# Loading and multiplying the gate matrix ahead of the query matrix in a one-token attention and GEGLU kernel

## The chip, the core and the metric

The kernel runs on one core of one Trainium2 chip. The metric is device time in microseconds (us) of one execution; lower is better. A core has a tensor engine (PE, with its weight loads shown apart as PEld), a vector engine (DVE), a scalar engine (ACT), a GpSimd engine (POOL) and a sync engine (SP). In this kernel SP only issues transfers from memory, in the order in which the program lists them, and 16 DMA engines carry them out.

## The reference, cut to what matters

Eight tokens (one for each batch entry, 512 wide) are normalised, and the normalised `xn` goes two ways. One is attention over the last 1024 positions of a cache of 8 key/value heads, with 32 query heads of 128. The other is a GEGLU block with 1792 hidden columns. The second gates the first.

```
xn = layernorm(x)                                   # 8 x 1 x 512
q  = xn @ wq                                        # 512 x 4096
p  = softmax(q . k_cache[last 1024] * 128**-0.5)    # 8 batches, 8 kv heads
s  = (p @ v_cache[last 1024]) @ wo                  # 4096 x 512
g  = silu((gelu(xn @ w_gate) * (xn @ w_up)) @ w_down)
out = x + s * g
```

All tensors are bf16. Key and value windows are 2 MB for each head, so 32 MB of them are read; `wq` and `wo` are 4 MB each, and `w_gate`, `w_up` and `w_down` are 1.8 MB each. That is 47.5 MB read for a very small amount of arithmetic for each byte.

## The kernel before, in words

**Buffers and transfers.** Every large operand lands in one of nine equal buffers called `big` (16 KB in each of 128 partitions, L69). They are used in turn, so the tenth tile takes the buffer of the first, and its transfer waits until the first tile has been read for the last time. All of these transfers are issued by SP in program order: `wq` in three transfers (L141 to L150: rows k=0, k=1, and k=2 and 3 together), then the gate matrix, the up matrix, key heads 0 to 2, the down matrix, value head 0, and from then on key and value heads in turn, last `wo` in seven pieces. `load_rows` (L92) loads a whole weight matrix with four consecutive rows for each partition: for the gate and up matrices this is one run of 4 x 1792 bf16 values, 14336 bytes, in each partition. A row of `wq` is a run of 8192 bytes; the third `wq` transfer has runs of 16384 bytes. The small input `x` is issued by ACT (L90).

**The opening.** `x` is normalised on DVE and ACT (L176 to L188), turned into columns on PE (L194), and copied into two padded layouts: `xqT`, by DVE (L197), which the query products use, and `xnT`, by ACT (L201), which the gate and up products use. Then come the query products (L311), 32 matmuls into two PSUM tiles `sc` and `o_ps`, in the order of the four row groups k; two casts each by DVE (L318) and ACT (L322) into `q_row`; `spread_x` (L218), which puts `x` into the layout of the output; the gate products (L359, w = 0), 16 matmuls into PSUM tile `s`; `turn_queries` twice (L328), 16 transposes on PE and eight copies in turn by DVE and ACT into `qT`; `masks` (L254) on DVE; and the up products (L359, w = 1) into `o_ps`. All of it stands in one hand-written order; each engine runs its instructions in that order.

**The loop.** L578 runs over steps of half a set (a set is half a head's batches): keys are transposed on PE (L439) and copied out by DVE and ACT in turn (L450, L452), scores are formed (L461), softmax follows (L469 to L504), values are multiplied nine steps later (L515), and `gather` (L526) normalises a head. The GELU of the gate result is spread over the first loop steps (`hidden_steps`, L374), two of its operations a step. `wo` is multiplied last (L621, L629), and the output is formed by two DVE operations (L657, L658).

**Transfer waits.** A transfer on SP also waits for the eighth transfer before it (that on ACT counted) to have landed, beside the wait for its buffer.

Of the kernel before, what the change touches and what calls it, by code (L numbers as in the profile page):

```python
# [12 lines left out]
FP32 = mybir.dt.float32  # L13
# [4 lines left out]
def kernel(  # L18
# [13 lines left out]
    nc = tc.nc  # L32
# [7 lines left out]
    F = B_w_gate.shape[1]  # L40
    NDC = D // 128
    NFC = F // 128
    scale = float(Dh) ** -0.5
    P = nc.NUM_PARTITIONS
# [17 lines left out]
    NQB = D // 128  # L62
# [15 lines left out]
    ps_o = ctx.enter_context(tc.tile_pool(name="ps_o", bufs=1, space=PSUM))  # L78
    ps_s = ctx.enter_context(tc.tile_pool(name="ps_s", bufs=1, space=PSUM))
# [12 lines left out]
    def load_rows(w, r0, n, per, name):  # L92

        t = big.tile([P, 2 * SET], BF16, name="big")
        cols = w.shape[1]
        nc.sync.dma_start(  # L96
            out=t[:, 0 : n * cols],
            in_=w.rearrange("(p k) n -> p k n", p=P)[:, r0 : r0 + n, :],
        )
        return t[:, 0 : n * cols].rearrange("p (k n) -> p k n", k=n)  # L100
# [24 lines left out]
    def load_wo(h, r0, n, nh=1):  # L125

        t = wo_at(h)[:, h % HB : h % HB + nh, r0 * D : (r0 + n) * D]
        nc.sync.dma_start(
            out=t if nh > 1 else t[:, 0, :],
            in_=A_wo[h * rep * Dh : (h + nh) * rep * Dh, :].rearrange(  # L130
                "(h p r) n -> p h (r n)", p=P, r=rep
            )[:, :, r0 * D : (r0 + n) * D]
            if nh > 1
            else A_wo[h * rep * Dh : (h + 1) * rep * Dh, :].rearrange(
                "(p r) n -> p r n", r=rep
            )[:, r0 : r0 + n, :],
        )
        return [t[:, i, :].rearrange("p (r n) -> p r n", r=n) for i in range(nh)]

    wq_rows = []  # L140
    for k0, cuts in ((0, (1, 1)), (2, (2,))):  # L141
        t = big.tile([P, 2, Hq * Dh], BF16, name="big")
# [60 lines left out]
    def xn(k):  # L203

        return xnT[:, k, :, :].rearrange("p b f -> p (b f)")
# [12 lines left out]
    def spread_x():  # L218

        ps = m_top[0:32, :]  # L220
        for q in range(NQB):
            nc.tensor.matmul(
                ps, sel[:, PB - q : PB - q + 32], x_sb[:, q * 128 : (q + 1) * 128],
                start=(q == 0), stop=(q == NQB - 1),
            )
        nc.vector.tensor_copy(out=xf, in_=ps)
# [27 lines left out]
    def masks():  # L254
        nc.vector.tensor_reduce(
            out=parts, in_=identf.rearrange("p (x n) -> p n x", n=NC),
            axis=AX.X, op=ALU.max,
        )
        nc.vector.tensor_reduce(
            out=gsel, in_=parts.rearrange("p (g j) -> p g j", j=rep),  # L260
            axis=AX.X, op=ALU.max,
        )
        nc.vector.tensor_reduce(
            out=half, in_=identf.rearrange("p (r c n) -> p c r n", c=2, n=NC),
            axis=AX.XY, op=ALU.max,
        )
        nc.vector.tensor_reduce(
            out=quarter[:, PB:], in_=identf.rearrange("p (a k) -> p k a", k=32),
            axis=AX.X, op=ALU.max,
        )  # L270

        nc.vector.tensor_scalar(
            out=gsel, in0=gsel, scalar1=-1.0, scalar2=-NEG, op0=ALU.add, op1=ALU.mult
        )
        nc.vector.tensor_copy(
            out=own.rearrange("p c b g -> p (c b) g"),
            in_=gsel.unsqueeze(1).to_broadcast([P, CP * 32 // G, G]),
        )

        m = small.tile([P, NC], FP32, name="m16")  # L280
        nc.vector.tensor_scalar(
            out=m, in0=parts, scalar1=-1.0, scalar2=-NEG, op0=ALU.add, op1=ALU.mult
        )
        nc.vector.tensor_copy(
            out=same, in_=m.unsqueeze(1).to_broadcast([P, NR * 2, NC])
        )
        for c in range(2):
            for b in range(2):
                nc.vector.tensor_scalar(
                    out=sums[:, c, b].rearrange(  # L290
                        "p j (g y) f -> p y j g f", y=NB
                    )[:, b],
                    in0=parts.rearrange("p (g j) -> p j g", j=rep)
                    .unsqueeze(3).to_broadcast([P, rep, G, PB]),
                    scalar1=half[:, c : c + 1], scalar2=None, op0=ALU.mult,
                )
# [2 lines left out]
    g_sb = rows.tile([32, 128], FP32, name="g_sb")  # L299

    NT = Hkv // NQB
    HD = rep * Dh
    q_ps = [ps_sc.tile([P, HD], FP32, name="sc"), ps_o.tile([P, HD], FP32, name="o_ps")]
    for k in range(NDC):
        w = wq_rows[k]
        for t in range(NT):
            for g in range(NQB):
# [4 lines left out]
                    start=(k == 0), stop=(k == NDC - 1), skip_group_check=True,  # L314
# [13 lines left out]
    def turn_queries(t):  # L328

        ps = ps_kT.tile([P, rep, 2, P], BF16, name="kT_ps")  # L330
        for j in range(rep):
            for e in range(2):
                nc.tensor.transpose(
                    ps[:, j, e, :],
                    q_row[:, t, j, e].rearrange("p c w -> p (c w)"),
                    ident,
                )
        for e in range(2):
            for c in range(2):
                out = qT[c * DP : (c + 1) * DP, e, t * NQB * NB : (t + 1) * NQB * NB, c]  # L340
                in_ = ps[c * DP : (c + 1) * DP, :, e].rearrange(
                    "p j (s g f) -> p s g j f", g=G, f=PB
                )[:, :, :, :, 0]
                if c == 0:
                    nc.vector.tensor_copy(out=out, in_=in_)
                else:
                    nc.scalar.activation(out=out, in_=in_, func=ACT.Copy)


    FG = F // NQB  # L350
    zu = [ps_s.tile([P, FG], FP32, name="s"), ps_o.tile([P, FG], FP32, name="o_ps")]
    spread_x()
    KW = NDC
    for w, src in enumerate((B_w_gate, B_w_up)):
        for k0 in range(0, NDC, KW):
            wt = load_rows(src, k0, KW, NDC, "gu")
            for k in range(KW):
                for g in range(NQB):
                    nc.tensor.matmul(  # L359
                        zu[w][32 * g : 32 * g + 32, :], xn(k0 + k),  # L360
                        wt[:, k, g * FG : (g + 1) * FG],
                        start=(k0 + k == 0), stop=(k0 + k == NDC - 1),
                        skip_group_check=True,
                    )
            if w == 0 and k0 == 0:
                for t in range(NT):
                    turn_queries(t)
                masks()
    zT, uT = zu
    z2 = rows.tile([P, FG], FP32, name="z2")  # L370


# [135 lines left out]
    o_ps = {}  # L508
# [69 lines left out]
    for t in range(2 * NS + LV + 3):  # L578
        s, i = divmod(t, 2)
# [62 lines left out]
    for n, (h0, r0, nr, nh) in enumerate(pieces):  # L642
        t = load_wo(h0, r0, nr, nh)
# [6 lines left out]
        if n == 2:  # L650

            nc.tensor.matmul(
                l_ps, pick, s_sb, start=False, stop=False, skip_group_check=True
# [38 lines left out]
```

## Time and profile before

| | |
|---|---|
| median of 3 runs | 120.66 us (120.48 to 121.86) |
| the profiled execution | 120.43 us |
| its span in the profile | 118.7 us |
| bytes read | 47.46 MB, 400 GB/s over the span |
| PE busy | 83.3 us (70%) |
| DVE busy | 65.1 us (55%) |
| ACT busy | 56.2 us (47%) |
| POOL busy | 6.7 us (6%) |

The span reaches from the first to the last thing that the profile records; the execution's own time is 1.7 us longer. Busy shares are averages over the whole span. "Busy" for the DMA engines is the mean over the sixteen of them. Lines such as L359 are lines of the kernel before. In a list by time, each row has its start, how long it (or the merged run of equal instructions) took, the engine, the line, the operation and its tiles, and in brackets how long the engine stood idle before it and what ended that.

### The profile page before, as it was taken

How to read it: one execution, taken by the hardware profiler on the slowest of the kernel's cores; microseconds unless marked ns; L12 is line 12 of the kernel's file. 1: busy time of each engine (PE TensorE's matmuls, PEld its weight loads, DVE VectorE, ACT ScalarE, POOL GpSimd, SP SyncE). 2: the span in 40 equal slices, each digit the busy share in tenths (PEclk: the TensorE clock that was granted, in tenths of full speed). 3: DMA queues.
4: the chain of work that ended last, by engine and by line, in shares of the span. 5: the costliest groups of instructions: out<-in, count | busy, mean ns of one | idle time of the engine just before them, and what ended most of it. 6: DMA issues, size and time to landing. Idle time of an engine off the chain costs nothing.

```text
span 118.7 us, 2391 instructions
## 1 busy us (share of the span) xinstructions
PE 83.3 (70%) x976; PEld 58.6 (49%) x976; DVE 65.1 (55%) x172; ACT 56.2 (47%) x94; POOL 6.7 (6%) x29
## 2 busy tenths in 40 slices
PE   0070639519956399699999969787795988776390
PEld 0020216119743366377677547555573755555380
DVE  0410131812799899648678658485673955734301
ACT  0500030204961887838685884676565577232000
POOL 7400000000000000000000000000000000000000
PEclk9999999999999999999999999999999999999999
DMA  3999999999999999999999999999999999999950
GB/s 99 425 450 442 401 449 403 431 431 423 423 453 414 423 425 425 428 420 428 428 431 420 425 428 425 420 431 425 425 431 428 420 428 434 413 416 420 410 192 3
DMA packets 6825, 47.60 MB, mean 401 GB/s; under 512 B 536, under 2 KB 800, under 8 KB 1952
## 3 DMA queue, kind: packets, MB, share of 16 engines
q1 hardware_dynamic: 6752, 47.45, 95.3%
q8 instruction: 7, 0.11, 0.3%
q10 hardware_dynamic: 64, 0.02, 0.1%
q14 instruction: 2, 0.02, 0.0%
HBM read 47.46 MB, written 0.01 MB: 400 GB/s over the span
## 4 chain that ended last, share of the span: by engine, by line
DMA 73%; PE 10%; DVE 8%; ACT 3%; SPq 2%; issue 1%
DMA big<-in_A_k_cache_dram 47%; DMA big<-in_A_wo_dram 26%; PE kT_ps L439 6%; PE sc L629 2%; DVE h_row L387 2%; DVE sc_sb L469 1%; DVE pT L504 1%; ACT L380 1%; SPq L145 1%; DVE kT L450 1%; SPq L96 1%; ACT kT L452 1%; PE s L407 1%; ACT p L494 1%; PE sc L461 1%
## 5 line engine op out<-in xcount | busy, mean ns | idle before, releaser
L452 ACT ACTIVATE kT<-kT_ps 128x1024 bf16<-128x1024 bf16 x32 | 32.4, 1020 | 23.4 <-PE kT_ps L439 23.2
L439 PE MATMUL kT_ps<-identf,big 128*128 128x128 f32 x256 | 37.7, 292 | 6.7 <-DMA big<-in_A_k_cache_dram 6.7
L439 PEld LDWEIGHTS kT_ps<-identf,big 128*128 128x128 f32 x256 | 30.1, 149 | 14.2 <-DMA big<-in_A_k_cache_dram 8.5
L450 DVE COPY kT<-kT_ps 128x1024 bf16<-128x1024 bf16 x32 | 22.0, 688 | 15.9 <-PE kT_ps L439 15.6
L494 ACT ACTIVATE p<-sc_sb,bias 128x512 bf16<-128x512 f32 x16 | 11.5, 718 | 6.7 <-DVE bias L485 6.3
L515 PE MATMUL o_ps<-big,pT 128*32 128x256 bf16 x256 | 12.5, 274 | 2.7 <-ACT blk L522 1.5
L504 DVE STREAM_TRANSPOSE pT<-p 128x512 bf16<-128x512 bf16 x16 | 11.3, 705 | 2.6 <-ACT p L494 2.4
L480 PE MATMUL m_ps<-identf,top 128*128 128x128 f32 x32 | 7.3, 310 | 5.9 <-DVE top L469 4.1
L469 DVE CUSTOM_DVE_ANT_0 sc_sb<-sc,own 128x512 f32<-128x512 f32 x16 | 10.5, 654 | 0.0
L461 PE MATMUL sc<-kT,zeros 128*32 128x512 bf16 x128 | 10.0, 388 | 0.5 <-ACT kT L452 0.5
L515 PEld LDWEIGHTS <-pT 128*32 128x32 bf16 x256 | 5.8, 94 | 7.6 <-issue 1.9
L532 PE MATMUL m_ps<-blk,sums 128*128 128x129 f32 x64 | 9.3, 286 | 0.0
L480 PEld LDWEIGHTS m_ps<-identf,top 128*128 128x128 f32 x32 | 4.7, 187 | 8.1 <-DVE top L469 4.9
L532 PEld LDWEIGHTS m_ps<-blk,sums 128*128 128x128 f32 x64 | 8.1, 191 | 0.9 <-issue 0.2
L498 POOL COPY blk<-blk 128x1 f32<-128x1 f32 x16 | 2.9, 183 | 97.3 <-ACT p L494 97.3
L522 ACT ACTIVATE blk<-o_ps 128x256 f32<-128x256 f32 x16 | 6.1, 382 | 3.0 <-PE o_ps L515 3.0
L311 PE MATMUL sc<-big,zeros 128*32 128x512 bf16 x16 | 2.5, 612 | 4.3 <-DMA big<-in_A_wq_dram 3.9
L318 DVE CAST q_row<-sc 128x512 bf16<-128x512 f32 x2 | 1.3, 686 | 7.5 <-PE sc L311 7.5
L485 DVE CUSTOM_DVE_ANT_0 scr<-m_ps,same 128x128 f32<-128x128 f32 x16 | 4.6, 289 | 1.4 <-PE m_ps L480 1.4
L322 ACT ACTIVATE q_row<-o_ps 128x512 bf16<-128x512 f32 x2 | 1.1, 594 | 7.6 <-PE o_ps L311 7.6
L194 PE MATMUL s<-ident,xhat 8*128 8x8 bf16 x4 | 0.3, 174 | 6.2 <-DVE xhat L185 6.2
L311 PEld LDWEIGHTS <-zeros 128*32 128x32 bf16 x32 | 1.1, 120 | 6.4 <-issue 5.8
(77 smaller groups left out, 61.0 us busy)
## 6 DMA issues: line engine op xcount, KB each, us to landing
big<-in_A_k_cache_dram SPq DMA_DIRECT2D x8, 2048.0 KB, 33.0
big<-in_A_v_cache_dram SPq DMA_DIRECT2D x7, 2048.0 KB, 33.7
big<-in_A_wq_dram SPq DMA_DIRECT2D x2, 1024.0 KB, 5.7
big<-in_A_wq_dram SPq DMA_DIRECT2D x1, 2048.0 KB, 11.2
big<-in_A_v_cache_dram SPq DMA_DIRECT2D x2, 1024.0 KB, 28.9
big<-in_A_wo_dram SPq DMA_DIRECT2D x1, 2048.0 KB
big<-in_B_w_gate_dram SPq DMA_DIRECT2D x1, 1792.0 KB, 15.0
big<-in_B_w_up_dram SPq DMA_DIRECT2D x1, 1792.0 KB, 18.5
```

What stands on the lines that cost most here:

```text
L439: nc.tensor.transpose(ps[:, c, :], K[s][:, 2 * (i * QP + c) : 2 * (i * QP + c) + 2, :] .rearrange("p c d -> p (c d)").bitcast(FP32), identf,)
L450: nc.vector.tensor_copy(out=out, in_=in_)
L452: nc.scalar.activation(out=out, in_=in_, func=ACT.Copy)
L461: nc.tensor.matmul(ps[32 * R : 32 * R + 32], qT[:, e, s].rearrange("p c b j -> p (c b j)"), t[:, :, 32 * R : 32 * R + 32, e], start=(e == ...
L469: nc.vector.tensor_tensor_reduce(out=sc[s], in0=ps.rearrange("p c k -> p (c k)"), in1=own.rearrange("p c b g -> p (c b g)"), op0=ALU.add, ...
L480: nc.tensor.matmul(ps, top.pop(s).to_broadcast([P, P]), identf, start=True, stop=True)
L485: nc.vector.tensor_tensor_reduce(out=scr, in0=ps, in1=same.rearrange("p x n -> p (x n)"), op0=ALU.add, op1=ALU.min, scale=-scale, scalar=- ...
L494: nc.scalar.activation(out=P_[s], in_=sc.pop(s), func=ACT.Exp, scale=scale, bias=biases.pop(s), accum_out=blk[s][:, 0, Dh : Dh + 1],)
L504: nc.vector.transpose(out=pT[s].rearrange("p c k -> p (c k)"), in_=P_.pop(s))
L515: nc.tensor.matmul(o_ps[s][32 * q : 32 * q + 32].rearrange("p c d -> p (c d)"), pT[s][:, c, :], V[s][:, 2 * c : 2 * c + 2, :].rearrange("p ...
L522: nc.scalar.activation(out=blk[s][:, :, 0:Dh], in_=o_ps.pop(s), func=ACT.Copy)
L532: nc.tensor.matmul(ps, sums[:, c, b].rearrange("p j b f -> p (j b f)"), t[:, c, :], start=(b == 0 and c == 0), stop=(b == NB - 1 and c == 1),)
```

## The change

The gate matrix becomes the first large transfer that SP issues, ahead of the three `wq` transfers, and it takes the first of the nine buffers. Its 16 products are put ahead of the query products on PE, and its PSUM tile `s` is claimed there. The up products keep their place behind `masks`, and the order of the transfers behind `wq` (up matrix, keys) stays. The matmul loop becomes a function that both products call; the instructions themselves, their number and their sizes stay the same. The transfer of the gate matrix is the same as before too: one transfer of 128 runs of 14336 bytes.

```diff
+    gate_w = load_rows(B_w_gate, 0, NDC, NDC, "gu")
     wq_rows = []
     for k0, cuts in ((0, (1, 1)), (2, (2,))):
         t = big.tile([P, 2, Hq * Dh], BF16, name="big")
...
+    FG = F // NQB
+
+    def zu_products(ps, wt):
+        for k in range(NDC):
+            for g in range(NQB):
+                nc.tensor.matmul(
+                    ps[32 * g : 32 * g + 32, :], xn(k),
+                    wt[:, k, g * FG : (g + 1) * FG],
+                    start=(k == 0), stop=(k == NDC - 1), skip_group_check=True,
+                )
+
+    zT = ps_s.tile([P, FG], FP32, name="s")
+    zu_products(zT, gate_w)
...
-
-    FG = F // NQB
-    zu = [ps_s.tile([P, FG], FP32, name="s"), ps_o.tile([P, FG], FP32, name="o_ps")]
     spread_x()
-    KW = NDC
-    for w, src in enumerate((B_w_gate, B_w_up)):
-        for k0 in range(0, NDC, KW):
-            wt = load_rows(src, k0, KW, NDC, "gu")
-            for k in range(KW):
-                for g in range(NQB):
-                    nc.tensor.matmul(
-                        zu[w][32 * g : 32 * g + 32, :], xn(k0 + k),
-                        wt[:, k, g * FG : (g + 1) * FG],
-                        start=(k0 + k == 0), stop=(k0 + k == NDC - 1),
-                        skip_group_check=True,
-                    )
-            if w == 0 and k0 == 0:
-                for t in range(NT):
-                    turn_queries(t)
-                masks()
-    zT, uT = zu
+    for t in range(NT):
+        turn_queries(t)
+    masks()
+    uT = ps_o.tile([P, FG], FP32, name="o_ps")
+    zu_products(uT, load_rows(B_w_up, 0, NDC, NDC, "gu"))
     z2 = rows.tile([P, FG], FP32, name="z2")
```

## Prediction, made blind

> **What bounds the kernel now.** I read the page's row of slices first, then busy time by stage, then the opening, and the end.
>
> ```profile
> DMA  3999999999999999999999999999999999999950
> GB/s 99 425 450 442 401 449 403 431 431 423 423 453 414 423 425 425 428 420 428 428 431 420 425 428 425 420 431 425 425 431 428 420 428 434 413 416 420 410 192 3
> DMA 73%; PE 10%; DVE 8%; ACT 3%; SPq 2%; issue 1%
> ```
>
> The first row is the busy share of the DMA engines in 40 slices of 2.97 us, the second what they moved, the third the engines' shares of the chain that ended last. From the second slice to the 38th the transfers never pause. Busy time by stage (after the window and its length: busy time of PE, PEld, DVE, ACT, POOL, granted PE clock, DMA share, GB/s) cuts the span at the places that matter:
>
> ```profile
> 0.00:1.50 1.50, 0.00 (x0) 0.00 (x0) 0.00 (x0) 0.00 (x0) 0.90 (x7) 1.00 0.00 0
> 1.50:3.00 1.50, 0.00 (x0) 0.00 (x0) 0.05 (x1) 0.00 (x0) 1.50 (x6) 1.00 0.77 208
> 3.00:26.00 23.00, 9.96 (x88) 4.22 (x88) 6.59 (x25) 3.95 (x9) 1.38 (x3) 1.00 1.01 428
> 26.00:112.00 86.00, 70.38 (x822) 51.86 (x823) 57.62 (x144) 52.23 (x85) 2.94 (x16) 1.00 1.01 425
> 112.00:115.20 3.20, 2.42 (x59) 2.09 (x59) 0.29 (x1) 0.00 (x0) 0.00 (x0) 1.00 0.72 267
> 115.20:118.70 3.50, 0.58 (x11) 0.40 (x8) 0.56 (x2) 0.00 (x0) 0.00 (x0) 1.00 0.01 2
> ```
>
> So the span is three things: a head until the transfers run at full rate, 109 us of transfers at 425 to 428 GB/s, and a tail of 3.5 us behind the last packet. Between 3 and 112 us the DMA engines are full (share 1.01) and no engine's work changes what they move. The change moves no byte of the sum; it can act on the head, or it must make the queue of transfers run dry, or make the last computation late.
>
> **The head.** The first `wq` packet starts at 1.70 us in the records of packets, after SP's first issue, which began at 0.73 us and took 0.36. From 1.5 to 3.0 us only 208 GB/s x 1.5 us = 0.31 MB move, which at 428 GB/s would be 0.73 us; so the transfers behave as if they had started at full rate at 3.00 - 0.73 = 2.27 us, and 0.57 us are lost after the first packet. The first sixteen packets of 8 KB took 0.38 to 1.0 us each, later ones 0.31 us.
>
> **The opening's computation.** The list by time of before:
>
> ```profile
> 12.85 0.62 PE L311 MATMUL sc<-big,zeros 128*32 128x512 bf16 x4 [3.86 <-DMA big<-in_A_wq_dram]
> 17.18 1.69 PE L359 MATMUL s<-big,zeros 128*32 128x448 bf16 x16 [1.90 <-DMA big<-in_B_w_gate_dram]
> 18.80 1.89 PE L333 MATMUL kT_ps<-ident,q_row 128*128 128x128 bf16 x16
> 21.32 1.68 PE L359 MATMUL o_ps<-big,zeros 128*32 128x448 bf16 x16 [0.63 <-DMA big<-in_B_w_up_dram]
> 23.87 0.25 DVE L289 TENSOR_SCALAR sums<-parts,half 128x64 f32<-128x64 f32 x1
> 26.21 5.38 PE L439 MATMUL kT_ps<-identf,big 128*128 128x128 f32 x24 [3.21 <-DMA big<-in_A_k_cache_dram]
> 27.37 0.69 DVE L450 COPY kT<-kT_ps 128x1024 bf16<-128x1024 bf16 x1 [3.24 <-PE kT_ps L439]
> 31.53 0.77 PE L461 MATMUL sc<-kT,zeros 128*32 128x512 bf16 x8
> ```
>
> Each stage waits for a transfer, and before the keys PE stands idle 3.21 us and DVE 3.24 us. These are the covers that the moved work may use up.
>
> **What the change does, part by part.** The 14 KB runs are no new thing: the packets of before already hold 384 of 14336 bytes (gate, up and down matrix, 128 each), at 0.535 us each. What changes is only who is first.
>
> *The transfers' landings.* With 0.428 MB a us from 2.27 us, `wq` (4.19 MB) ends at 12.1, gate (6.03 MB) at 16.4, up (7.86 MB) at 20.6, key head 0 (9.96 MB) at 25.5 us; the waits above end at 12.85, 17.18, 21.32 and 26.21, so 0.7 to 0.8 us lie between last byte and use. After the change, by the same sum: gate (1.84 MB) usable at about 7.3 us, `wq` row 0 at 9.8, row 1 at 12.2, rows 2 and 3 at 17.2, up and keys as now at 21.3 and 26.2.
>
> *PE and the others.* The gate products (1.69 us) run from 7.3, since `xnT` is there after ACT's copy at 6.91 + 0.24 = 7.15; they end at 9.0, ahead of `wq` row 0. The 16 query products of rows 2 and 3 run from 17.2. In before the first DVE cast came 1.52 us after 12.85 and took 1.29 for two; now 18.7 to 20.0. ACT's came 1.94 us after and took 1.08; now 19.1 to 20.2. `spread_x` (0.60) fits between on PE. The transposes of the queries, which before found their casts long done, now wait for them: 20.0 to 21.9 us. DVE's first copy of them came 1.08 us after their start, and the eight alternating copies took 2.06 us: 21.1 to 23.2. The masks took 2.56 us (21.56 to 24.12): now about 22.8 to 25.4. The up products go from 21.9, behind the transposes, to 23.6. So the opening ends about 1.3 us later on DVE, with 2.0 us left to its first key copy at 27.37, and on PE 2.6 us remain to the keys at 26.21. The rotated queries are first used at 31.53, 8 us after they are there. Cost: nothing, hidden by the wait for key head 0; without that cover it is 1.3 us of computation, and the end has room for that too (below).
>
> *SP's queue.* These are its rows of before:
>
> ```profile
> 5.43 0.57 SPq L96 DMA_DIRECT2D big<-in_B_w_down_dram  x1
> 7.91 7.82 SPq L107 DMA_DIRECT2D big<-in_A_v_cache_dram  x1
> 15.85 5.60 SPq L107 DMA_DIRECT2D big<-in_A_k_cache_dram  x1
> 21.55 4.50 SPq L107 DMA_DIRECT2D big<-in_A_v_cache_dram  x1
> 26.14 4.93 SPq L107 DMA_DIRECT2D big<-in_A_k_cache_dram  x1
> ```
>
> The down matrix waits for the first transfer's landing, now the gate's at 7.3 instead of 5.4 us, and value head 0 for the second's, now 9.8 instead of 7.9; behind these on SP stand only transfers. Up to the down matrix 16.0 MB are queued by then, of which 3.2 have moved by 9.8 us, so 12.8 MB, some 30 us of transfers, are still to come. Key head 3 now takes the gate's buffer (free at 9.0), value head 1 that of `wq` rows 0 and 1 (12.2 + about 0.9), key head 4 that of rows 2 and 3 (19.0): each before SP comes to it (15.85, 21.55, 26.14), where the issues of 4.5 to 7.8 us already show SP held by a full queue. Cost: nothing; if this cover went, a late issue would have to use up those 30 us of queue first.
>
> *The first issue and the ramp.* This is the only place with a price. The first issue would take between 0.36 us (the row of the first one now) and 0.69 us (the gate's own row, third in line behind others); the up matrix, the same shape, took 0.44. I take that: +0.08, ends 0 and +0.33. If the time to the first byte hangs on the start of an issue rather than its end, it is 0. The Trainium skill, "DMA: Bandwidth & Descriptors", section on latency and other measured facts, gives about 600 ns to the first byte for transfers issued from SP; the trace agrees if it is counted from the issue's end, 1.70 - 1.09 = 0.61 us, and by that rule the 0.69 us issue would cost the full +0.33. The ramp's loss of 0.57 us was not seen with 14 KB packets. If it is a fixed latency on the first packets of each engine it stays (0); if it grows with the packet it is 14/8 of it, +0.43; if it is a pace in packets, the same packets carry 14/8 of the bytes, 0.55 MB in the ramp, nearly the full rate, and the gain is about 0.55. I take 0, since the first packets took up to 0.7 us more than later ones while the rows of each size at full rate cost alike (0.311 us for 8 KB, 0.535 for 14 KB), which looks like a latency and not a rate.
>
> *The tail.* The end of before:
>
> ```profile
> 109.95 0.75 DVE L550 STREAM_TRANSPOSE oL<-o 128x128 bf16<-128x128 bf16 x1
> 112.75 0.63 PE L621 MATMUL s<-big,oR 128*32 128x128 bf16 x32 [1.37 <-DMA big<-in_A_wo_dram]
> 113.38 0.61 PE L629 MATMUL sc<-big,oL 128*32 128x128 bf16 x8
> ```
>
> Attention's last operand is ready at 110.7 and first used at 113.38, when `wo` has landed: 2.7 us of room. Nothing here moves except with the transfers.
>
> **Sum.** +0.08 against the profiled execution of 120.43 gives 120.5; the median of the runs is 0.23 above that execution, and the same change on it gives 120.7. I say **120.6**. Two per cent, 2.4 us, is about what a measurement of this kernel can tell from no change, so this is a forecast of no change.
>
> **Rivals.** (1) *The start gains*: the ramp is paced by packets, -0.55, so 119.9 (120.1 on the median). For it: 14 KB of `w_gate` follow each other without holes, while a `wq` row is read in 8 KB pieces 32 KB apart. Against: later `wq` packets show no such penalty. (2) *The start loses*: long issue and growing ramp, +0.76, so 121.2 (121.4 on the median). For it: the gate's own issue row of 0.69. (3) *The queries come too late*: the computation would become the bound. DVE has 2.0 us before the keys and the end 2.7, so it decides only from 4.7 us beyond my sum for the opening, and costs over 2% (above 122.8, say 123.5) from 7.1 us beyond. For it: PE is busy for all 5 us from 27 to 32, so a lost microsecond isn't regained at once. Against: PE waits for keys again later, 1.27 us at 90.69, so the computation has caught up by then. (4) *The transfers were not the bound*, and PE's idle 3.86 and 1.90 us now filled bring a gain of a like size, 5.8 us at most, 114.6 to 118: the full DMA rows speak against it. That the change doesn't do what it says would leave 120.4 to 120.7, as forecast.
>
> **Chances.** Forecast (within 0.4 us of 120.6) 0.55; (1) 0.19; (2) 0.16; (3) 0.06; (4) 0.04. Within 2% are the first three, 0.90; slower 0.06, faster 0.04. The range takes in both ends of the ramp and issue, on the lower and the upper base, and some of the spread of the runs shown (up to 121.86): 119.7 to 121.9.
>
> **What would show it.** Right: transfers at 425 to 428 GB/s from about 3 us on, key head 0 used near 26.2 us, first key copy near 27.4, the same tail. The gate products start near 7.3 us, the query transposes near 20.0, the masks end near 25.4. Wrong: a slice with DMA below 9 in the middle, keys that PE takes up late, or attention's end (110.7) past the landing of `wo`.

## The result, and the profile after

| | before | changed |
|---|---|---|
| median of the runs | 120.66 us | 121.62 us |
| ratio changed / before | | 1.0092, 95% interval 1.0067 to 1.0117 |
| the profiled execution | 120.43 us | 121.63 us |
| its span | 118.7 us | 119.8 us |
| PE busy / DVE busy | 83.3 / 65.1 us | 86.0 / 65.5 us |
| packets, bytes read | 6825, 47.46 MB | 6825, 47.46 MB |

The changed kernel is 0.9% slower, clear of its interval, inside the range that was given (119.7 to 121.9) but not the "no change" that was forecast. The runs of most kernels here, the one before included, fall into two groups some 1.2 us apart (in the profiled runs of the upper groups the clock granted to PE is 0.50 at the end, as the last section shows; that the others have the same cause is inferred), so where a median falls between the groups, the lower group is compared with that of before (120.4 to 120.8 us).

The slices of the changed kernel, from its page:

```profile
DMA  4999999999999999999999999999999999999920
GB/s 103 393 418 438 435 426 421 425 427 430 408 441 441 415 424 421 435 427 424 419 432 432 419 427 419 427 430 432 416 432 427 427 430 421 412 424 417 396 105 3
```

The transfers still never pause. The second and third slices lie lower, 393 and 418 against 425 and 450 GB/s; behind them the slices of both kernels scatter (401 to 453 in before). Busy time by stage, cut finer at the head; first the changed kernel (after the window and its length: busy time of PE, PEld, DVE, ACT, POOL, granted PE clock, DMA share, GB/s):

```profile
1.50:3.00 1.50, 0.00 (x0) 0.00 (x0) 0.32 (x1) 0.00 (x0) 1.50 (x6) 1.00 0.90 206
3.00:9.00 6.00, 0.87 (x12) 0.55 (x16) 1.38 (x6) 1.82 (x3) 1.37 (x3) 1.00 0.96 404
9.00:26.00 17.00, 9.13 (x80) 3.80 (x72) 4.66 (x18) 2.14 (x6) 0.00 (x0) 1.00 1.01 429
26.00:112.00 86.00, 72.45 (x798) 53.56 (x802) 57.38 (x145) 52.25 (x85) 2.94 (x16) 0.94 1.01 425
```

and the same two stages of the kernel before:

```profile
9.00:26.00 17.00, 7.62 (x68) 3.44 (x67) 4.95 (x19) 2.13 (x6) 0.00 (x0) 1.00 1.00 426
3.00:9.00 6.00, 2.34 (x20) 0.78 (x21) 1.65 (x6) 1.82 (x3) 1.38 (x3) 1.00 1.03 436
```

From 9 us on the rates are alike (429 and 426, then 425 and 425). From 3 to 9 us the changed kernel moves 404 instead of 436 GB/s, 0.19 MB less, which is 0.45 us. From then on everything is late. The changed kernel by time:

```profile
8.42 1.69 PE L308 MATMUL s<-big,zeros 128*32 128x448 bf16 x16 [2.22 <-DMA big<-in_B_w_gate_dram]
20.96 1.89 PE L349 MATMUL kT_ps<-ident,q_row 128*128 128x128 bf16 x16 [0.43 <-DVE q_row L334]
25.54 0.73 DVE L290 TENSOR_SCALAR sums<-parts,half 128x64 f32<-128x64 f32 x4
27.22 4.29 PE L440 MATMUL kT_ps<-identf,big 128*128 128x128 f32 x24 [2.75 <-DMA big<-in_A_k_cache_dram]
28.37 0.69 DVE L451 COPY kT<-kT_ps 128x1024 bf16<-128x1024 bf16 x1 [2.10 <-PE kT_ps L440]
...
113.87 0.63 PE L622 MATMUL s<-big,oR 128*32 128x128 bf16 x32 [1.34 <-DMA big<-in_A_wo_dram]
114.51 0.61 PE L630 MATMUL sc<-big,oL 128*32 128x128 bf16 x8
```

PE takes up the keys at 27.22 instead of 26.21, still after a wait for their transfer, and the last products at 113.87 instead of 112.75, again after a wait for theirs. So a microsecond is lost before the keys, in the transfers, and it is still there at the end. But 0.45 us is not 1.0. The rest is seen only when the sixteen DMA engines are looked at one by one. Each transfer ends on each of its engines with a write of 4 bytes, and the trace records these writes; sixteen of them end a transfer of 128 partitions. The records do not name the engines; an engine is followed by its lag behind the first one, which repeats from transfer to transfer, mostly within 0.03 us. Times of these records are counted here from the start of the span, as in the lists (the prediction's are about 0.06 us too early: its first packet, at 1.70 us there, starts at 1.76). The times of the writes for three transfers, and the end of the last data packet of the kernel:

| transfer | before: first engine, median, last | changed: first engine, median, last |
|---|---|---|
| key head 0 | 25.43, 25.71, 25.87 | 25.61, 25.90, 26.87 |
| key head 7 | 88.49, 88.91, 90.23 | 88.67, 89.48, 91.35 |
| first `wo` transfer | 108.17, 108.81, 109.92 | 108.35, 109.16, 110.85 |
| last data packet of all | 115.04 | 116.15 |

In the changed kernel the first engine is 0.2 us later throughout, the last one about 1.0. PE takes up the keys behind the last engine: 0.34 us after it in before (26.21) and 0.35 in the changed kernel (27.22). In before all sixteen ended key head 0 within 0.45 us; in the changed kernel three engines trail the rest, at 26.83, 26.85 and 26.87, and one more at 26.35. These times, here and below, are those of one profiled execution of each kernel.

### The profile page after: what moved, and what is told of

Same layout as the page of the kernel before. It is cut to its first block, busy times and chain, and to the rows that moved or that the text cites. A ratio compares the mean times of both kernels' runs of the same rounds, so it can differ in the third digit from the quotient of the medians.

```text
span 119.8 us, 2391 instructions
## 1 busy us (share of the span) xinstructions
PE 86.0 (72%) x976; PEld 60.8 (51%) x976; DVE 65.5 (55%) x172; ACT 56.2 (47%) x94; POOL 6.7 (6%) x29
## 2 busy tenths in 40 slices
DMA packets 6825, 47.60 MB, mean 397 GB/s; under 512 B 536, under 2 KB 800, under 8 KB 1952
## 3 DMA queue, kind: packets, MB, share of 16 engines
HBM read 47.46 MB, written 0.01 MB: 396 GB/s over the span
## 4 chain that ended last, share of the span: by engine, by line
DMA 46%; PE 36%; DVE 7%; ACT 4%; issue 2%; SPq 2%
DMA big<-in_A_wo_dram 26%; DMA big<-in_A_k_cache_dram 20%; PE kT_ps L440 18%; PE sc L462 5%; PE o_ps L516 4%; PE m_ps L481 3%; PE m_ps L533 2%; PE sc L630 2%; DVE h_row L388 2%; ACT kT L453 2%; SPq L146 1%; ACT L381 1%; DVE sc_sb L470 1%; DVE o L540 1%; PE m_ps L419 1%
## 5 line engine op out<-in xcount | busy, mean ns | idle before, releaser
L440 PE MATMUL kT_ps<-identf,big 128*128 128x128 f32 x256 | 39.6, 302 | 4.9 <-DMA big<-in_A_k_cache_dram 4.9
L440 PEld LDWEIGHTS kT_ps<-identf,big 128*128 128x128 f32 x256 | 31.9, 155 | 12.8 <-DMA big<-in_A_k_cache_dram 6.2
L462 PE MATMUL sc<-kT,zeros 128*32 128x512 bf16 x128 | 10.7, 413 | 0.8 <-ACT kT L453 0.5
L481 PEld LDWEIGHTS m_ps<-identf,top 128*128 128x128 f32 x32 | 5.2, 204 | 8.3 <-DVE top L470 5.2
```

The source lines that it names most:

```text
L440: nc.tensor.transpose(ps[:, c, :], K[s][:, 2 * (i * QP + c) : 2 * (i * QP + c) + 2, :] .rearrange("p c d -> p (c d)").bitcast(FP32), identf,)
L462: nc.tensor.matmul(ps[32 * R : 32 * R + 32], qT[:, e, s].rearrange("p c b j -> p (c b j)"), t[:, :, 32 * R : 32 * R + 32, e], start=(e == ...
L481: nc.tensor.matmul(ps, top.pop(s).to_broadcast([P, P]), identf, start=True, stop=True)
```

## The experiments

The theory formed from this (called S before its details were clear): at the very start single engines are held up in their first packets of the gate matrix; every engine has a fixed sixteenth of each transfer, so its lag stays with it to the last packet. Rivals: P, the new order of the products on PE; M, the gate matrix's place in memory; L, the run length of 14336 bytes; X, the load of `x` beside it.

**The order of the products alone.** The transfers as before, the products as after (`gate_w` is loaded behind the three `wq` transfers):

```diff
-    gate_w = load_rows(B_w_gate, 0, NDC, NDC, "gu")
     wq_rows = []
...
         wq_rows += [t[:, i : i + 1, :] for i in range(2)]
+    gate_w = load_rows(B_w_gate, 0, NDC, NDC, "gu")
```

> The transfers in the order of before, the products in the order of the changed kernel (gate products ahead of the query products, so that PE waits for the gate matrix near 17.2 us and the queries come still later than in the changed kernel, masks to about 29). Theories S and M: the transfers decide, 120.7, key head 0 landed as before. Theory P: 121.6 or more, as the changed kernel.

Measured: 120.65 us median, ratio 0.9992 (0.9944 to 1.0039). The list by time of this run:

```profile
17.19 1.69 PE L309 MATMUL s<-big,zeros 128*32 128x448 bf16 x16 [10.96 <-DMA big<-in_B_w_gate_dram]
23.02 1.07 PE L350 MATMUL kT_ps<-ident,q_row 128*128 128x128 bf16 x16 [0.86 <-DVE q_row L335]
26.25 1.97 PE L441 MATMUL kT_ps<-identf,big 128*128 128x128 f32 x16 [1.28 <-DMA big<-in_A_k_cache_dram]
27.15 0.74 DVE L291 TENSOR_SCALAR sums<-parts,half 128x64 f32<-128x64 f32 x4
```

PE idles 10.96 us for the gate matrix, the query transposes start 2.1 us later than in the changed kernel, and the masks end at 27.89, later than the keys. It costs nothing: the keys are taken up at 26.25, as before, and DVE's first key copy, 0.43 us late at 27.80, leaves no trace in the time. P is out, and the cover that the prediction relied on is shown, with more weight on it than the change puts there.

**Other matrices and run lengths first.** Seven kernels vary what is loaded first. `up_first` exchanges the two matrices, `wq_row_first` puts one transfer of `wq` ahead of the gate matrix; `gate_7k` and `gate_3k` cut the gate matrix into two and four transfers by rows; `wq_16k` and `wq_14k` are the kernel before with longer first runs; `warm` puts 64 KB in small runs first.

```diff
# up_first
-    gate_w = load_rows(B_w_gate, 0, NDC, NDC, "gu")
+    up_w = load_rows(B_w_up, 0, NDC, NDC, "gu")
...
-    uT = ps_o.tile([P, FG], FP32, name="o_ps")
-    zu_products(uT, load_rows(B_w_up, 0, NDC, NDC, "gu"))
+    zT = ps_o.tile([P, FG], FP32, name="o_ps")
+    zu_products(zT, load_rows(B_w_gate, 0, NDC, NDC, "gu"))
# wq_row_first
-    gate_w = load_rows(B_w_gate, 0, NDC, NDC, "gu")
...
             i += n
+            if k0 == 0 and i == 1:
+                gate_w = load_rows(B_w_gate, 0, NDC, NDC, "gu")
# gate_7k; gate_3k with (1, 1, 1, 1)
-    gate_w = load_rows(B_w_gate, 0, NDC, NDC, "gu")
...
+    for n in (2, 2):
+        nc.sync.dma_start(
+            out=gate_w[:, k0 : k0 + n, :],
+            in_=B_w_gate.rearrange("(p k) n -> p k n", p=P)[:, k0 : k0 + n, :],
+        )
+        k0 += n
# wq_16k, on the kernel before
-    for k0, cuts in ((0, (1, 1)), (2, (2,))):
+    for k0, cuts in ((0, (2,)), (2, (2,))):
# wq_14k, on the kernel before: cuts are elements of the flattened two rows
+    for k0, cuts in ((0, (7168, 1024)), (2, (8192,))):
...
+            nc.sync.dma_start(out=flat[:, a : a + n], in_=src[:, a : a + n])
# warm
+    warm = rows.tile([P, 256], BF16, name="warm")
+    nc.sync.dma_start(
+        out=warm, in_=A_wq.rearrange("(p k) n -> p k n", p=P)[:, 0, 0:256]
+    )
```

> The changed kernel with the up matrix loaded and multiplied first and the gate matrix in the up matrix's place: the same shape, the same runs of 14336 bytes, other memory. Theory G (any matrix that is read first in runs of 14336 bytes that follow one another without holes): 121.6, spread of the engines' ends at the first matrix 1.0 us or more. Theory M (the place of the gate matrix in memory): 120.7, spread about 0.5.

> The changed kernel with the first row group of the query matrix (1 MB in runs of 8192 bytes) ahead of the gate matrix, the other two transfers of the query matrix behind it. If only the very start is harmful to the 14336-byte runs: the engines end the gate matrix within 0.5 us, as in the kernel before, 120.7. If this matrix is slow whenever it comes within the first microseconds, as behind the 64 KB of the warm-up run: 121.4 to 121.6.

> The gate matrix is still first, but in two transfers of two rows for each partition (runs of 7168 bytes, where the changed kernel has one transfer with runs of 14336). Theory S (the first packets of each DMA engine are slow, the more so the longer they are; the engine that comes out last keeps its lag, since each engine has a fixed sixteenth of every transfer): the lag goes, the key head 0 is used near 26.3 us and the time is within 0.3 us of before, about 120.7. Theory M (the gate matrix's own addresses are slow when they are read first, in any run length): 121.6, key head 0 near 27.2. Theory P (the order of the products on PE, queries late): 121.6.

> The changed kernel with the gate matrix first in four transfers of one row for each partition (runs of 3584 bytes). If runs of 14336 bytes that follow without holes are what stalls single engines at the start: no engine stalls, spread 0.5 us after the first transfer, and the time is 120.7 to 121.0, as with 7168. If shorter runs cost at the start by themselves (more packets, more semaphore writes), it's above the run with 7168: 121.0 to 121.3.

> The kernel before with its order of transfers and products, but the first two rows of the query matrix in one transfer with runs of 16384 bytes instead of two with 8192. Theory S: first packets of 16 KB lag as those of 14 KB do, or more: 121.6 to 121.9, key head 0 used near 27.2 us or later. Theory M: the query matrix isn't the gate matrix, about 120.7. Theory P: the products keep their order, 120.7.

> The kernel before with its order, but the first two row groups of the query matrix cut differently: a first transfer with runs of 14336 bytes (a row and three quarters of the next), then the remaining 2048 bytes of each partition. Theory L (the run length of 14336 bytes itself, whatever the matrix): 121.4 to 121.6, spread 1.0 us or more after the first transfer. Theory G (runs that follow without holes): as the run with 16384-byte runs, 120.7 to 120.8, spread 0.5.

> The changed kernel with one small transfer ahead of the gate matrix: 128 runs of 512 bytes of the query matrix (64 KB, 0.15 us at full rate) into a tile that nothing reads. If a DMA engine is slow in its first packets whatever they read (one form of S), the small packets take the slow start and the gate's follow at full rate: 120.7 to 121.0, key head 0 near 26.3 to 26.5. If it's the first reads of a region of memory that are slow, or M, the gate's packets are as late as in the changed kernel: 121.6 to 121.9.

Measured (times: median, ratio with interval, lower group of the runs; then, from the trace, the ends of key head 0 on the first and the last engine and the last data packet, in us; the last column is the longest first packet in ns):

| run | median | ratio | lower group | key head 0: first, last engine | last packet | longest |
|---|---|---|---|---|---|---|
| before | 120.66 | | 120.4 to 120.8 | 25.43, 25.87 | 115.04 | 995 |
| changed | 121.62 | 1.0092 (1.0067 to 1.0117) | 121.4 to 121.6 | 25.61, 26.87 | 116.15 | 2340 |
| up_first | 120.92 | 1.0021 (0.9982 to 1.0060) | 120.7 to 121.2 | 25.64, 26.82 | 115.45 | 1428 |
| wq_row_first | 120.56 | 0.9979 (0.9938 to 1.0019) | 120.5 to 120.9 | 25.62, 25.94 | 115.22 | 1155 |
| gate_7k | 121.45 | 1.0048 (0.9998 to 1.0099) | 120.8 to 120.9 | 25.64, 26.20 | 115.46 | 1040 |
| gate_3k | 121.85 | 1.0116 (1.0078 to 1.0154) | 121.3 to 121.5 | 25.72, 26.26 | 115.54 | 822 |
| wq_16k | 120.72 | 1.0006 (0.9967 to 1.0046) | 120.6 to 120.8 | 25.52, 25.99 | 115.22 | 1407 |
| wq_14k | 120.69 | 0.9992 (0.9957 to 1.0027) | 120.6 to 120.8 | 25.61, 25.94 | 115.17 | 1445 |
| warm | 122.10 | 1.0120 (1.0035 to 1.0204) | 122.0 to 122.1 | 26.18, 27.50 | 116.58 | 1855 |

What follows, one by one:

- *L falls.* The query matrix first in runs of 14336 or 16384 bytes keeps all engines within 0.5 us and costs nothing. The expectation of the first form of S, that long first packets lag by their length, falls with it: the first sixteen packets of 16 KB take 0.6 to 1.4 us (0.61 later), and yet all engines end together.
- *Shorter runs of the same matrix take the stall away.* With 7168 and 3584 bytes no engine trails by a microsecond (spread 0.56 and 0.54 us). What remains is 0.2 to 0.4 us by which all engines are later, and in time 0.25 us (7168) to 0.7 us (3584: 121.3 and 121.5, at and just above its second expectation). Why 3584 costs more than 7168, with nearly the same ends at key head 0, stays open.
- *M holds only in part.* The up matrix first, of the same shape, stalls one engine (26.82; the next ends at 26.36), where the gate matrix stalls three by a microsecond and one by half of that. Its time is only 0.25 us above before. So it has the spread that theory G foretold and nearly the time of theory M. A reason is given below.
- *Only the start is harmful*: with 1 MB of `wq` ahead of it, the gate matrix ends on all engines within 0.33 us, and the kernel is as fast as before. The start is more than the engines' first packets, though: behind 64 KB in 512-byte runs, which were done at 2.31 us, the gate matrix still stalls three engines, which end key head 0 by 1.1 to 1.3 us behind the first. A warm engine doesn't help; `warm` fell on the side of "the first reads of a region, or M", with its lower runs at 122.0 to 122.1 us even above what was foretold there (121.6 to 121.9); its first engine, too, ends key head 0 later by 0.57 us than that of the changed kernel.

**The load of x.** The eight packets of `x` are served at the same time, at 1.70 to 2.33 us. Issued by SP ahead of the gate matrix they are out of the way:

```diff
-    nc.scalar.dma_start(out=x_sb, in_=A_x.flatten_outer_dims())
+    nc.sync.dma_start(out=x_sb, in_=A_x.flatten_outer_dims())
```

> The changed kernel with the small input x issued by SP ahead of the gate matrix instead of by ACT beside it. Theory X (the gate's first packets are held up on the engines that at the same time serve x from ACT's queue): the lag goes, all sixteen engines end the gate matrix within about 0.5 us of each other (1.3 in the changed kernel), time 120.7 to 120.9 plus about 0.1 for the issue of x. Any theory in which the gate's own transfer is slow at the start: spread stays at 1.0 us or more, 121.6 to 121.8.

Measured: 122.56 us median of four runs (121.9, 122.1, 123.0, 123.2), ratio 1.0148 (1.0080 to 1.0216). The first gate packet starts at 2.16 us instead of 1.76, which puts the lower runs above what was foretold (121.6 to 121.8), and three engines end the gate matrix 0.8 to 1.0 us behind the median, as in the changed kernel. X is out.

**Does one engine's lag reach the end?** The kernel before, with an extra transfer that only one engine carries (23 runs have no common divisor with 16), and two controls in which all engines take an equal part. The records bear this out: the extra transfer ends with one write of 4 bytes in the first case and with sixteen in the controls. The extra tile is read by nobody.

```diff
         wq_rows += [t[:, i : i + 1, :] for i in range(2)]
+    side = rows.tile([23, 1056], BF16, name="side")      # side_all: 32, 760; side_even: 16, 1056
+    nc.sync.dma_start(
+        out=side,
+        in_=A_wo.rearrange("(p r) n -> p (r n)", r=rep)[0:23, 0:1056],
+    )
```

> The kernel before with one more transfer behind the query matrix: 23 runs of 2112 bytes (48.6 KB) into a tile that nothing reads; 23 has no common divisor with 16, so they should all go to one DMA engine, 1.9 to 2.0 us of its time at 40 ns a KB. Theory S' (each engine has a fixed share and carries its lag to the end): that engine ends key head 0 and every later transfer 1.9 us behind the others, key head 0 is used near 28.0 us, and the end moves by 0.8 us (the lag less the 1.1 us by which the last engine trails the median in before anyway) to 1.9 us (if this engine also gets one of the instruction loads): 121.5 to 122.6. If engines shared the work out among themselves: +0.12, 120.8.

> The same 48.6 KB, cut into 32 runs of 1520 bytes, so that all sixteen engines take a part: 0.12 us of each. Both theories: 120.7 to 120.8. It is the control for the run with one engine (its issue and its bytes without the lag).

> A second control for the run with one engine, after the first one (32 runs of 1520 bytes) was slow for a reason of its own: all later packets took 11% longer from 12 to 31 us. Here 16 runs of 2112 bytes, the run length of the one-engine transfer, one for each engine (33.8 KB, 0.09 us of each). If any extra small transfer in this place slows the later packets: 122 or more, 8 KB packets at 0.34 us. If the 1520-byte runs were the cause: 120.6 to 120.8, packets at 0.31 us, and the 0.8 us of the one-engine run are its lag.

Measured, side_one: 122.18 us median of four runs in two groups (121.4 and 121.6; 122.8 and 123.0), ratio 1.0129 (1.0067 to 1.0192). The lower group is 0.9 us above that of before. PE and DVE at the keys, and the stage in which nearly all bytes move:

```profile
28.28 4.10 PE L445 MATMUL kT_ps<-identf,big 128*128 128x128 f32 x18 [3.91 <-DMA big<-in_A_k_cache_dram]
29.43 0.69 DVE L456 COPY kT<-kT_ps 128x1024 bf16<-128x1024 bf16 x1 [3.27 <-PE kT_ps L445]
```

```profile
3.00:26.00 23.00, 9.02 (x88) 3.94 (x88) 6.18 (x25) 3.92 (x9) 1.38 (x3) 0.99 1.01 425
26.00:112.00 86.00, 71.11 (x822) 52.53 (x823) 57.90 (x146) 52.18 (x85) 2.94 (x16) 0.94 1.01 425
```

The mean rate is that of before, 425 GB/s, and yet the keys come 2.07 us later than before (26.21). The records show why: the sixteenth engine ends key head 0 at 27.86 us, the fifteenth at 26.01. The lag is 1.85 us, near the 1.9 worked out, and it doesn't shrink: behind the first engine it is 2.24 us at key head 0 (27.86 - 25.62) and 2.22 at the first `wo` transfer (110.60 - 108.38), whose last engine in before came at 109.92. The last packet of the kernel ends at 115.72, 0.68 after that of before. That is near the expectation's lower bound (0.8), the lag less the trailing that is there anyway. Had the engines shared the work, 48.6 KB would have cost 0.12 us.

The Trainium skill, "DMA: Bandwidth & Descriptors", in its section on the iDMA fabric, says in passing, within an explanation that it calls unconfirmed, that a bulk load runs at the pace of its slowest engine. The trace of side_one agrees, with 1.85 us at key head 0, and adds that the engine stays behind to the end.

The first control did not control: side_all took 123.64 us (1.0213, 1.0150 to 1.0276). Its lag is nil, but its row of slices shows another loss:

```profile
GB/s 107 424 443 412 425 385 390 359 387 387 403 427 449 413 419 430 422 422 430 430 424 424 427 430 427 422 427 424 430 427 419 430 427 422 419 419 420 384 53 3
```

From the sixth to the tenth slice (15 to 30 us) the transfers run at 359 to 390 GB/s: packets of 8 KB take 0.343 us instead of 0.309, those of 14 KB 0.596 instead of 0.535, all alike, until about 32 us. In the second control, side_even, two runs were at 120.8 us, as expected, and two at 124.1; the profiled one is of the first kind, with 8 KB packets at 0.309 us. No trace shows what slowed the other two, so it stays open whether 1520-byte runs are needed for the loss. The two runs at 120.8 show that an extra transfer in this place, with its issue, need not cost more than 0.2 us, and side_one's own trace shows 8 KB packets at 0.309 us throughout; this is why its 0.7 us can be read as the lag's.

## Why the prediction failed, point by point

- **What bounds the kernel: right.** 425 to 429 GB/s from 9 to 112 us in both kernels; the added PE idling in pe_order_only cost nothing.
- **The opening: right in its order and its cover**, with all its times late by the transfers' delay. Foretold and measured: gate products 7.3 and 8.42, query transposes 20.0 and 20.96, masks' end 25.4 and 26.27, keys 26.2 and 27.22, first key copy 27.4 and 28.37; DVE still waited 2.10 us before it, as foretold (2.0). Of the signs of being wrong that were named, one came: the keys that PE takes up late.
- **SP's queue: right.** The down matrix was issued at 8.30 and value head 0 at 10.71 us, later than before (5.43, 7.91), and the DMA row shows no gap.
- **The first issue: right.** It took 0.37 us (0.07 less than allowed for), and the first packet started at 1.76 us in both kernels. The figure of the Trainium skill that was weighed there ("DMA: Bandwidth & Descriptors", latency and other measured facts, about 600 ns to the first byte) is a little low if counted from the issue's end: 1.76 - 1.10 = 0.66 us here and 1.76 - 1.09 = 0.67 in before, not the 0.61 of the prediction. The issue of 0.69 us, by which it would have cost 0.33, did not come.
- **The ramp: the step that failed.** I took 0 from a range of -0.55 to +0.43, arguing from a latency common to all first packets, and counted the sixteen engines as one pool ("the transfers behave as if they had started at full rate at 2.27 us"). By that mean the loss is 2.79 - 2.47 = 0.32 us (full-rate start from the bytes moved by 9.5 us, from the packets' records), inside the range. The 2.27 us of the prediction was early for before as well, since the windows count a packet whole at its start; and the 0.7 to 0.8 us that it set between last byte and use shrink to 0.34 when the last engine is taken. The keys and the end wait for the slowest engine, and that lost 1.0: two first packets took 2.3 us where the longest in before took 1.0 (the third engine's delay is not seen in one packet). Neither the mean nor the range had a place for that.
- **The tail: right in itself** (attention's operand was ready at 112.90 and used at 114.51), but "nothing here moves except with the transfers" hid that the transfers' own tail is one engine's. How the lag gets there shows in the table of the first section. In before the last engine trails the first by 0.45 us at key head 0 and by 1.74 at key head 7 and 1.75 at the first `wo` transfer. In the changed kernel it is 1.26, 2.68 and 2.50. What lies between are the engines' turns at loading instructions, which the page of either kernel lists as a queue of their own:

```profile
q8 instruction: 7, 0.11, 0.3%
```

These are seven packets of 16 KB, 0.88 to 0.97 us each, in both kernels, and behind each of the first six one engine's lag has jumped. In before every one hits another engine: six lags between 1.41 and 1.75 us stand at the first `wo` transfer, and none above (two more loads, of 8 KB, leave lags of 1.00 and 0.84). In the changed kernel the three engines held up at the start are spared until key head 6; the six largest lags behind the first engine are then 1.24, 1.26, 1.43, 1.52, 1.68, 1.73. The load at 88.7 us hits one of the three: at key head 7 the 1.26 is gone and 2.68 is there. The load at 102.8 hits the next: at the first `wo` transfer the other one, 1.22, is gone too, and 2.49 and 2.50 stand at the end of the list. So the microsecond lost at the start is on top of the microsecond that every kernel here loses to its instruction loads. The other profiles bear this out: at the first `wo` transfer the largest lag is 2.49 us in `warm` and x_on_sp, which also have three engines held up, and 1.57 to 1.96 us wherever fewer or none were (side_one, whose lag was made, apart).
- **Why up_first escapes**: its one slow engine is 1.19 us behind the first at key head 0, and an unchanged 1.17 still stands among its lags at the first `wo` transfer. No load hit that engine; the largest lag there is 1.93 us, and the last packet is at 115.45 instead of 116.15. That three slow engines of sixteen are more often hit than one is argued from this, not tested; the changed kernel's lower group lay at 121.4 to 121.6 in all 13 of its runs.
- **The rivals.** (2), "the start loses", is what came, at 121.6 instead of 121.2 to 121.4 and by stalled engines instead of a long issue and a ramp in proportion to the packet. (1), (3) and (4) did not come. The reason given for (1), that the gate matrix's bytes follow one another without holes, points the wrong way, if anywhere: the same rows in 7168-byte runs with holes between them stall no engine.
- **What stays open**: why the first reads of the gate matrix in 14336-byte runs hold up three engines, those of the up matrix one, and those of the query matrix in runs of the same length none. It isn't the run length alone, not a cold engine, not `x`, not the products. The place in memory, the alignment of the runs and their packing were not separated. Theory G of the expectations, first reads of 14336-byte runs that follow one another without holes, fits the spreads of all runs here, but it doesn't say why three engines in one matrix and one in the other; a matrix in packed runs at another place, which could have tested it, was not run.

No variant beat the kernel before: wq_row_first, at 0.9979 (0.9938 to 1.0019), is the same within its interval.

## What to carry to other kernels

In a kernel that is bound by its transfers, the end belongs to the slowest DMA engine and not to the mean rate: a stall of one engine at the start is still there at the end, and costs what of it rises above the lags that the other engines gather on the way (0.7 us of 1.85 in side_one; 1.1 in the changed kernel, where an instruction load came on top of the 1.0). Read the spread of a transfer's sixteen ends early (0.45 us in the good kernel, 1.26 in the bad one) beside the mean GB/s, and keep a range for it when the first transfer is exchanged. What PE did while it waited for the transfers could be moved about freely here; what is read first has to be measured.

## What the runs showed of the hardware that was not expected

- Instruction loads ride on the same engines: seven packets of 16 KB, 0.88 to 0.97 us each, one engine at a time. After one of them that engine stays behind for the rest of the kernel, by 1.42 us more where it can be followed (1.26 to 2.68).
- All sixteen engines can fall into a slower pace together: 0.343 instead of 0.309 us for 8 KB, for some 19 us, behind one transfer of 48.6 KB in the profiled execution of side_all. The cause was not found.
- The clock granted to PE fell in many executions without touching the time (runs of before took 120.34 us at a mean clock of 0.94 and 120.56 at 1.00), but not where it fell at the very end. Busy time by stage of before:

```profile
113.00:116.00 3.00, 2.75 (x62) 2.25 (x50) 0.47 (x2) 0.00 (x0) 0.00 (x0) 1.00 0.43 153
```

and of wq_row_first, whose profiled execution took 121.67 us:

```profile
113.00:116.00 3.00, 3.00 (x52) 2.89 (x52) 0.29 (x1) 0.00 (x0) 0.00 (x0) 0.50 0.47 167
```

At a clock of 0.50 the last products become the end: the final 24 matmuls end at 117.0 instead of 115.8 us, although the last data packet came at 115.22 against 115.04. The profiled executions of gate_7k (122.0 us) and x_on_sp (123.0 us) show 0.50 there too.
